# An earlier Silu, an earlier scaling of beta, and block reads on another queue, in a DeltaNet and SwiGLU kernel

## The chip, the cores and the metric

The kernel runs on one core of a Trainium2 chip. The metric is the device time of one execution in microseconds (us). The kernel before was timed three times: 864.71, 864.77 and 868.80 us, with a median of 864.77 us. The profiled execution has a span of 866.4 us.

Five engines run side by side, each through its own instructions in order: TensorE (PE; its weight loads are listed apart as PEld), VectorE (DVE), ScalarE (ACT), GpSimd (POOL) and SyncE (SP). SP, ACT and POOL also start transfers (DMA), each on its own queue.

## The reference: a delta-rule recurrence, then a gated feed-forward layer

The first half is a recurrent attention over 4 batches with 8 heads, 768 tokens and head size 48. The second half is a SwiGLU layer over the 3072 resulting rows of width 384, with an inner width of 1536. All inputs are float32 or wider; the weights arrive as 64-bit numbers.

```python
k_n = k / (norm(k) + 1e-06)
for t in range(S):
    y[:, :, t] = q[:, :, t] @ state
    v_old = state^T k_n[:, :, t]
    state += beta[:, :, t] * outer(k_n[:, :, t], v[:, :, t] - v_old)
x  = y rearranged to (3072, 384)
xn = x / sqrt(mean(x * x) + 1e-06) * rms_g
g  = xn @ w_gate
out = (g * sigmoid(g) * (xn @ w_val)) @ w_out
```

The gate product `g` goes through Silu, the value product does not, and their product is what the last matrix multiplies.

## The kernel before: the parts that matter here

The sequence is cut into six chunks of 128 tokens; with four batches there are 24 units, unit n being chunk n // 4 and batch n % 4. For each chunk the kernel computes scores of keys and queries, inverts a small triangular matrix per block (`invert`), runs the recurrence (`recur`) and then the feed-forward layer for two pairs of batches (`ffn`). These routines are Python generators. A plan with a time for each of them takes them forward in turn, so that the work of one chunk's attention lies between the matrix products of another chunk's feed-forward layer.

```python
with tc.manual_schedule():
    first = recur(0, 1.2, begin())
    next(first)
    at(1, first)
    run_plan(60)      # every engine keeps the order written
run_plan()            # from here on the scheduler orders each engine's instructions
```

One step `f` of the feed-forward layer makes 128 of the 1536 inner columns. Gate and value go into the two halves of one PSUM tile of 2 KB in each partition, of which there are two.

```python
for f in range(f0, f1):
    p_gv = psum.tile([128, 2, TOK], FP32, name="p_gv", tag="gv", bufs=2)
    for i in range(2):                      # 0: gate, 1: value
        for t in range(KT):
            nc.tensor.matmul(p_gv[:, i], wgv_sb[...], xt[:, t], ...)
        yield 1
    sil = work.tile([128, TOK], FP32, name="sil")
    nc.scalar.activation(out=sil, in_=p_gv[:, 0], func=ACTF.Silu)
    h_f = work.tile([128, TOK], FP32, name="h_f", bufs=3)
    nc.vector.tensor_tensor(out=h_f, in0=sil, in1=p_gv[:, 1], op=ALU.mult)
    if last is not None:
        leave(f - 1, last)                  # p_o += h_f of the step before, times w_out
        yield 1
    last = h_f
yield 0.9
leave(f1 - 1, last)
```

The preparation of a unit ends with its scores, which ScalarE copies and VectorE masks, and with four transfers that gather the diagonal blocks. The inversion of a chunk begins with the scaling of beta.

```python
def prepare(n):
    norm_k(n, square_k(n, nc.scalar)); yield 4
    transpose(n, qpad[n % 2], Q0); ... yield 3
    transpose(n, kpad[n % NK], K0); yield 2
    score(n, ..., both); yield 1
    gather(n)                               # four ScalarE-issued transfers

def scale_beta(c):                          # four VectorE instructions
    nc.vector.tensor_scalar_add(nrm, nrm, 1e-6)
    nc.vector.reciprocal(krec, nrm)
    for i in range(2):
        nc.vector.tensor_tensor(out=beta_t[:, c], in0=beta_t[:, c], in1=krec, op=ALU.mult)

def invert(c, dt):
    clear_ttb()
    scale_beta(c)
    turn_beta(c)                            # p_nb on TensorE, then nbeta on VectorE
    for b in range(B):
        scale_v(B * c + b)                  # GpSimd
    yield dt
    for i in range(W - 1):                  # 31 steps of two VectorE instructions
        ...  # tmp = gblk * nbeta * ttb ; ttb += tmp
        yield dt
```

The weights are turned from 64-bit to 32-bit numbers in the first 160 us by `convert`, five VectorE instructions for each piece (`top`, `wgv_sb` and `wo_sb` in the profile). In chunk 0 the inverse blocks go through memory: `td` and `nd` are written and read back by `read_two`, for batches 0 and 1 first and for 2 and 3 later.

```python
# chunk 0 of recur, cut
corner(None, 0); corner(None, 1)
read_two(2, *inverses)          # eight reads of 64 KB, all issued by SyncE
fetch(nc.sync.dma_start)        # a piece of weights
for n in (2, 3): load_v(n)
load_k(B)
...                             # inner, outer
transpose_y(0, scale(*ys.pop(0)))
stay_warm(2)
transpose_y(1, scale(*ys.pop(1)))
convert(4)
yield
```

Of the kernel before, what the change touches and what calls it, by code (L numbers as in the profile page):

```python
# [10 lines left out]
FP32 = mybir.dt.float32  # L11
# [17 lines left out]
def kernel(  # L29
# [401 lines left out]
    def prepare(n):  # L431
        norm_k(n, square_k(n, nc.scalar))
        yield 4
        transpose(n, qpad[n % 2], Q0)
        if n + 2 < NU:
            load_q(n + 2)
        yield 3
        transpose(n, kpad[n % NK], K0)
        yield 2
        score(n, crossed((0, slice(0, 3)), (1, slice(1, 4))), both)  # L440
        yield 1
        gather(n)


    def score_part(n, first):
# [83 lines left out]
        nc.scalar.dma_start(out=nd, in_=gblk)  # L529
        return td, nd  # L530

    def read_two(n, td, nd):
        own = slice(n * H, (n + 2) * H)
        both = ((td, tt_all[:, own]), (nd, ne_2))

        for d, to in both[:: -1 if n > 0 else 1]:
            for a in range(NBLK):
                o, first = W * (a % 2), a * BH + n * H
                (nc.sync if n > 0 or a < 2 else nc.scalar).dma_start(
                    out=to[W * a : W * (a + 1), :, o : o + W],  # L540
                    in_=d[first : first + 2 * H].rearrange("h r j -> r h j"),
                )

    def invert(c, dt):
        clear_ttb()
        scale_beta(c)
        turn_beta(c)
        for b in range(B):
            scale_v(B * c + b)
        yield dt  # L550
        for i in range(W - 1):
            n = W - 1 - i
            shape = [128, i + 1, n]
            tmp_b = work.tile([128, W * W // 4], FP32, name="tmp")
            tmp = tmp_b[:, 0 : n * (i + 1)].rearrange("p (k j) -> p k j", j=n)
            nc.vector.scalar_tensor_tensor(  # L556
                out=tmp,
                in0=gblk[:, i, None, i + 1 :].to_broadcast(shape),
                scalar=nbeta[:, i : i + 1],
                in1=ttb[:, 0 : i + 1, i : i + 1].to_broadcast(shape),  # L560
                op0=ALU.mult,
                op1=ALU.mult,
            )
            to = ttb[:, 0 : i + 1, i + 1 :]
            nc.vector.tensor_tensor(out=to, in0=to, in1=tmp, op=ALU.add)  # L565
            yield dt
        td = dram.tile([128, W, W], FP32, name="td")
        nc.sync.dma_start(out=td, in_=ttb)

        nd = dram.tile([128, W, W], FP32, name="nd")  # L570
        nc.vector.tensor_tensor(
            out=gblk,
            in0=ttb.rearrange("p s m -> p m s"),
            in1=nbeta[:, :, None].to_broadcast([128, W, W]),
            op=ALU.mult,
        )
        nc.sync.dma_start(out=nd, in_=gblk)
        for b in range(B):
            for a in range(NBLK):
                o = W * (a % 2)  # L580
                nc.sync.dma_start(
                    out=tt[b][W * a : W * (a + 1), :, o : o + W],
                    in_=td[a * BH + b * H : a * BH + (b + 1) * H].rearrange("h r j -> r h j"),
                )
            for a in (0, 2):
                nc.sync.dma_start(
                    out=ne[W * a : W * (a + 1), b * H : (b + 1) * H],
                    in_=nd[a * BH + b * H : a * BH + (b + 1) * H].rearrange("h r j -> r h j"),
                )
        yield dt  # L590
# [13 lines left out]
    def recur(c, dt, inverses=None):  # L604
# [204 lines left out]
        if c == 0:  # L809

            halved = [halves(b) for b in units]
            next(halved[0])
            next(halved[1])
            next(halved[0])
            next(halved[1])
            corner(0, None)
            corner(1, None)
            convert(2)
            corner(None, 0)
            corner(None, 1)  # L820
            read_two(2, *inverses)
            fetch(nc.sync.dma_start)
            for n in (2, 3):
                load_v(n)
            load_k(B)
            convert(3)
            inner(0, None, 0)
            inner(1, None, 1)
            inner(None, 0, None)
            inner(None, 1, None)  # L830
            convert(1)
            u_0, u_1 = us[0], us[1]
            stay_warm(1)
            outer(None, 0)
            outer(None, 1)
            for i in range(4):
                fetch(nc.gpsimd.dma_start)
            convert(3)
            stay_warm(3)
            transpose_y(0, scale(*ys.pop(0)))  # L840
            stay_warm(2)
            transpose_y(1, scale(*ys.pop(1)))
            convert(4)
            yield
            update(0, u_0)
            scale_v(2)
            scale_v(3)
            mask_queries(2)
            yield dt
            update(1, u_1)  # L850
            reload()
            yield dt
            next(halved[2])
            mask_queries(3)
            yield dt
            next(halved[3])
            yield dt
            next(halved[2])
            yield dt
            corner(2, None)  # L860
            next(halved[3])
            yield dt
            corner(3, 2)
            yield dt
            inner(None, None, 2)
            corner(None, 3)
            yield dt
            inner(2, None, 3)
            yield dt
            inner(3, 2, None)  # L870
            yield dt
            u_2, u_3 = us[2], us[3]
            outer(None, 2)
            yield dt
            inner(None, 3, None)
            yield dt
            outer(None, 3)
            yield dt
            transpose_y(2, scale(*ys.pop(2)))
            yield dt  # L880
            transpose_y(3, scale(*ys.pop(3)))
            yield dt
            update(2, u_2)
            yield dt
            update(3, u_3)
            reload()
            return
# [30 lines left out]
    def scale(y, p_y, rs):  # L918
        nc.scalar.mul(y, p_y.rearrange("p h d -> p (h d)"), rs)
        return y  # L920
# [18 lines left out]
    def ffn(m, f0, f1):  # L939
        xt = xts[m] if f1 < FT else xts.pop(m)  # L940
        p_o = [psum.tile([128, DM], FP32, name="p_o", tag="out", bufs=2) for i in range(2)]

        def leave(f, h_f):
            for i in range(2):
                nc.tensor.matmul(  # L945
                    p_o[i],
                    h_f[:, i * C : (i + 1) * C],
                    wo_sb[:, f],
                    start=(f == f0),
                    stop=(f == f1 - 1),  # L950
                )

        last = None
# [4 lines that stand above are left out]
                    nc.tensor.matmul(  # L958
                        p_gv[:, i],
                        wgv_sb[:, i * KT + t, f * 128 : (f + 1) * 128],  # L960
                        xt[:, t],
                        start=(t == 0),
                        stop=(t == KT - 1),
                    )
                yield 1
            sil = work.tile([128, TOK], FP32, name="sil")
            nc.scalar.activation(out=sil, in_=p_gv[:, 0], func=ACTF.Silu)  # L967
            h_f = work.tile([128, TOK], FP32, name="h_f", bufs=3)
            nc.vector.tensor_tensor(out=h_f, in0=sil, in1=p_gv[:, 1], op=ALU.mult)  # L969
            if last is not None:  # L970
                leave(f - 1, last)
# [5 lines that stand above are left out]
            n = 2 * m + i  # L977
            if f0 == 0:
                o_sb = work.tile([128, DM], FP32, name="o_sb", bufs=4)
                nc.scalar.copy(o_sb, p_o[i])  # L980
            else:
                o_sb = halves.pop(n)
                nc.vector.tensor_tensor(out=o_sb, in0=o_sb, in1=p_o[i], op=ALU.add)
            if f1 < FT:
                halves[n] = o_sb
                continue
            c, b = divmod(n, B)
            tok0 = b * S + c * C
            nc.sync.dma_start(out=out[tok0 : tok0 + C, :], in_=o_sb)
        yield 0.1  # L990
# [16 lines left out]
    def begin():  # L1007
# [31 lines left out]
            keep_queries(n, score_part(n, Q0))  # L1039
        tops.append(shrink(raws[1]))  # L1040
        inverses = invert_halves()
        read_two(0, *inverses)
        stay_warm(4)
        stay_warm(8, ttb_all[:, 0:DM].rearrange("p (t m) -> p t m", m=128))
        mask_queries(0)
# [57 lines left out]
```

## Time and profile before

| engine | busy us | share of the span | instructions |
| --- | --- | --- | --- |
| PE | 832.2 | 96% | 8640 |
| PEld | 638.7 | 74% | 8640 |
| DVE | 411.9 | 48% | 1000 |
| ACT | 251.7 | 29% | 655 |
| POOL | 107.0 | 12% | 146 |

The share of an engine over the whole span hides its stages. In the page's 40 slices of 21.7 us the DVE stands at 7 to 9 tenths in the first eight slices and then falls to between 1 and 7, while the PE stands at 9 in nearly all. The groups of instructions that the change touches are these:

| group | count | mean of one | busy us |
| --- | --- | --- | --- |
| p_gv products, 128x256 (PE) | 1728 | 386 ns | 416.1 |
| p_o products, 128x384 (PE) | 576 | 502 ns | 217.7 |
| sil (ACT) | 144 | 383 ns | 55.1 |
| h_f (DVE) | 144 | 418 ns | 60.2 |

Each float32 product of the program is two instructions in the trace, so one step `f` has six instructions for the gate, six for the value and four for `p_o`. "Idle before" in a row of the timeline is the time for which the engine had nothing to run just before that instruction, and the arrow names what ended it.

### The profile page before, as it was taken

Reading aid. Unit: us, or ns where it says so; the run is one execution under the profiler, and the core shown is the slowest. Engines: PE = TensorE matmul, PEld = TensorE weight load, DVE = VectorE, ACT = ScalarE, POOL = GpSimd, SP = SyncE. Lnnn points to the kernel's source line nnn. Section 1 sums busy time; section 2 is a strip of 40 time slices with the busy share of each in tenths; the row PEclk is TensorE's granted clock in tenths of the full one; section 3 lists DMA queues with packets and bytes.
Section 4 is the critical chain, followed back from the end, with each engine's and each line's share of the span. In section 5 each row is a group of like instructions: output and inputs, shape, how many; then the busy total and the mean of one; then the engine's idle time right before and its main releaser. Section 6 shows DMA issues by size and latency. Waiting matters only on the chain.

```text
span 866.4 us, 20251 instructions
## 1 busy us (share of the span) xinstructions
PE 832.2 (96%) x8640; PEld 638.7 (74%) x8640; DVE 411.9 (48%) x1000; ACT 251.7 (29%) x655; POOL 107.0 (12%) x146
## 2 busy tenths in 40 slices
PE   7898979689999999999999999999999999999998
PEld 6576757467887777877777887777777777777776
DVE  7869969791443761343661442671333581220100
ACT  5344446003334113244113244112334112220101
POOL 6012433100230000230000230000130000000000
PEclk9969999899999999999999999999999999999999
DMA  8846345104221131221121222122121122000000
GB/s 152 231 99 211 121 122 144 31 24 90 48 62 34 32 84 28 48 62 32 31 83 32 43 61 37 31 78 38 39 57 19 31 71 35 2 20 0 19 1 18
DMA packets 152058, 52.01 MB, mean 60 GB/s; under 512 B 143616, under 2 KB 146688, under 8 KB 151968
## 3 DMA queue, kind: packets, MB, share of 16 engines
q1 hardware_dynamic: 124816, 36.95, 18.5%
q0 software_dynamic: 2080, 10.23, 3.5%
q10 hardware_dynamic: 25072, 3.54, 2.3%
q8 instruction: 68, 1.11, 0.5%
q14 instruction: 22, 0.18, 0.1%
HBM read 36.54 MB, written 14.16 MB: 59 GB/s over the span
## 4 chain that ended last, share of the span: by engine, by line
PE 79%; DVE 15%; issue 2%; ACT 2%; DMA 1%; POOL 1%; SPq 0%; DVEq 0%; ACTq 0%; POOLq 0%
PE p_gv L958 38%; PE p_o L945 18%; DVE tmp L556 4%; DVE ttb L565 3%; PE p_g L373 3%; PE p_y L715 3%; PE p_z L771 2%; PE p_t L357 2%; PE p_k L753 2%; PE p_y L753 2%; PE p_z L780 1%; PE p_x L789 1%; PE p_v L620 1%; PE p_w L627 1%; DVE h_f L969 1%
## 5 line engine op out<-in xcount | busy, mean ns | idle before, releaser
L958 PE MATMUL p_gv<-xt,wgv_sb 128*128 128x256 f32 x1728 | 416.1, 386 | 1.3 <-DVE xt L929 0.7
L958 PEld LDWEIGHTS p_gv<-xt,wgv_sb 128*128 128x128 f32 x1728 | 321.5, 191 | 66.0 <-issue 4.3
L945 PE MATMUL p_o<-wo_sb,h_f 128*128 128x384 f32 x576 | 217.7, 502 | 9.0 <-DVE h_f L969 9.0
L969 DVE TENSOR_TENSOR h_f<-sil,p_gv 128x256 f32<-128x256 f32 x144 | 60.2, 418 | 247.3 <-ACT sil L967 247.2
L967 ACT ACTIVATE sil<-p_gv 128x256 f32<-128x256 f32 x144 | 55.1, 383 | 335.8 <-PE p_gv L958 314.4
L945 PEld LDWEIGHTS p_o<-wo_sb,h_f 128*128 128x128 f32 x576 | 105.0, 192 | 61.2 <-DVE h_f L969 13.8
L556 DVE SCALAR_TENSOR_TENSOR tmp<-gblk,nbeta,ttb 128x31 f32<-128x31 f32 (+15 forms) x155 | 62.7, 405 | 4.7
L387 DVE TENSOR_TENSOR gp<-p_g,mask 64x128 f32<-64x128 f32 (+1 forms) x160 | 37.9, 277 | 43.2 <-ACT gp L383 38.7
L565 DVE TENSOR_TENSOR ttb<-ttb,tmp 128x31 f32<-128x31 f32 (+15 forms) x155 | 53.0, 342 | 4.9
L320 POOL TENSOR_TENSOR knrm<-ksum,half 128x8 f32<-128x8 f32 x24 | 41.8, 1741 | 71.0 <-DVE ksum L319 70.8
L914 POOL TENSOR_SCALAR ms<-ms 128x1 f32<-128x1 f32 x24 | 5.3, 221 | 312.0 <-ACT y L906 311.7
L362 ACT COPY kqt<-p_t 128x512 f32<-128x512 f32 x48 | 28.1, 585 | 24.9 <-PE p_t L357 24.2
L489 POOL MEMSET ttb<- 128x1024 f32 x6 | 5.7, 954 | 228.9 <-DMA td<-ttb 228.9
L771 PEld LDWEIGHTS p_z<-v_raw,tt 64*64 64x64 f32 x768 | 26.0, 142 | 9.2 <-issue 7.2
L373 PE MATMUL p_g<-kqt 64*64 64x192 f32 x640 | 31.7, 330 | 0.9 <-ACT gp L383 0.9
L640 ACT COPY vs<-p_v 32x256 f32<-32x256 f32 x48 | 17.4, 362 | 44.4 <-PE p_w L627 23.2
L780 PE MATMUL p_z<-u,x 64*64 64x48 f32 x384 | 28.8, 227 | 0.7 <-DVE u L801 0.6
L789 PE MATMUL p_x<-tt,gp 64*64 64x64 f32 x384 | 29.0, 229 | 0.2 <-issue 0.2
L771 PE MATMUL p_z<-v_raw,tt 64*64 64x48 f32 x768 | 29.2, 227 | 0.0
L373 PEld LDWEIGHTS p_g<-kqt 64*64 64x64 f32 x640 | 23.1, 132 | 8.1 <-issue 5.3
L715 PE MATMUL p_y<-u,gp 128*64 128x48 f32 x768 | 27.6, 228 | 0.0
L780 PEld LDWEIGHTS p_z<-u,x 64*64 64x64 f32 x384 | 25.7, 142 | 2.4 <-issue 1.3
(117 smaller groups left out, 784.1 us busy)
## 6 DMA issues: line engine op xcount, KB each, us to landing
kpad<-in_k_dram SPq DMA_DIRECT2D x24, 192.0 KB, 2.9
qpad<-in_q_dram SPq DMA_DIRECT2D x24, 192.0 KB, 2.9
v_raw<-in_v_dram SPq DMA_DIRECT2D x24, 192.0 KB, 2.9
out_dram<-o_sb SPq DMA_DIRECT2D x24, 192.0 KB, 1.9
gblk<-gd SPq DMA_DIRECT2D x6, 512.0 KB, 3.3
td<-ttb SPq DMA_DIRECT2D x6, 512.0 KB, 2.6
raw<-in_moe_w_val_dram POOLq DMA_DIRECT2D x8, 384.0 KB, 4.3
raw<-in_moe_w_out_dram POOLq DMA_DIRECT2D x8, 384.0 KB, 4.3
```

The costliest lines, as they stand in the source:

```text
L320: nc.gpsimd.tensor_tensor(out=norms[c][:, b * H : (b + 1) * H], in0=ksum, in1=half, op=ALU.pow)
L373: nc.tensor.matmul(to, pair[d, K1 if i else K0], pair[d, places], skip_group_check=True)
L387: nc.vector.tensor_tensor(out=to[p, :, place], in0=p_g[p, :, place], in1=mask[p, i, None].to_broadcast([p.stop, 2, HC]), op=ALU.mult,)
L556: nc.vector.scalar_tensor_tensor(out=tmp, in0=gblk[:, i, None, i + 1 :].to_broadcast(shape), scalar=nbeta[:, i : i + 1], in1=ttb[:, 0 : i ...
L565: nc.vector.tensor_tensor(out=to, in0=to, in1=tmp, op=ALU.add)
L715: nc.tensor.matmul(p_y[p, h], gp[b_y][:, h, HC * place : HC * (place + 1)], u[:, h], start=(c == 0 and h == 0), stop=True, skip_group_chec ...
L771: nc.tensor.matmul(p_zs[b_z][p, h], tt[b_z][p, h], r[p, h], start=(h == 0), stop=(p is lo), skip_group_check=True,)
L780: nc.tensor.matmul(p_zs[b_u][hi, h], x2s[b_u][:, h], us[b_u][lo, h], start=False, stop=True, skip_group_check=True,)
L945: nc.tensor.matmul(p_o[i], h_f[:, i * C : (i + 1) * C], wo_sb[:, f], start=(f == f0), stop=(f == f1 - 1),)
L958: nc.tensor.matmul(p_gv[:, i], wgv_sb[:, i * KT + t, f * 128 : (f + 1) * 128], xt[:, t], start=(t == 0), stop=(t == KT - 1),)
L967: nc.scalar.activation(out=sil, in_=p_gv[:, 0], func=ACTF.Silu)
L969: nc.vector.tensor_tensor(out=h_f, in0=sil, in1=p_gv[:, 1], op=ALU.mult)
```

## The change

There are three parts. The Silu of a step is issued straight behind its gate product, ahead of the value product, where it used to stand behind both. The scaling of a chunk's beta moves from the head of the inversion to the end of the preparation of the chunk's last unit, for every chunk from the second on. Of the eight block reads for batches 2 and 3 of the first chunk, SyncE keeps one, and ScalarE issues the other seven later, behind the scaling of `y`; `read_two` takes a list of queues for that. The first part is to have the Silu done while TensorE works on the value product; the second is to have beta ready when the inversion asks for it; the third is to free SyncE's queue earlier for the transfers behind the reads.

```diff
 # prepare
         yield 1
         gather(n)
+        if n % B == B - 1:
+            scale_beta(n // B)
 # read_two: takes queues; None leaves a read out, and a short list ends it
-    def read_two(n, td, nd):
+    def read_two(n, td, nd, queues):
 # invert
         clear_ttb()
-        scale_beta(c)
         turn_beta(c)
 # recur, chunk 0
             corner(None, 1)
-            read_two(2, *inverses)
+            read_two(2, *inverses, [nc.sync])
             fetch(nc.sync.dma_start)
 ...
             transpose_y(1, scale(*ys.pop(1)))
+            read_two(2, *inverses, [None] + 7 * [nc.scalar])
             convert(4)
 # ffn
                         stop=(t == KT - 1),
                     )
+                if i == 0:
+                    sil = work.tile([128, TOK], FP32, name="sil")
+                    nc.scalar.activation(out=sil, in_=p_gv[:, 0], func=ACTF.Silu)
                 yield 1
-            sil = work.tile([128, TOK], FP32, name="sil")
-            nc.scalar.activation(out=sil, in_=p_gv[:, 0], func=ACTF.Silu)
             h_f = work.tile([128, TOK], FP32, name="h_f", bufs=3)
 # begin: the same queues as before
-        read_two(0, *inverses)
+        read_two(0, *inverses, 2 * [nc.sync, nc.sync, nc.scalar, nc.scalar])
```

The order of the reads in `read_two(2, ...)` is as before: the four of `nd` first, then the four of `td`.

More of the change, by code (lines that the diff above doesn't have):

```diff
@@ L530, in invert_halves @@
         return td, nd
-    def read_two(n, td, nd):
+    def read_two(n, td, nd, queues):
         own = slice(n * H, (n + 2) * H)
[L534 to L542, printed above, removed]
+        reads = [(d, to, a) for d, to in ((td, tt_all[:, own]), (nd, ne_2)) for a in range(NBLK)]
+        if n > 0:
+            reads = reads[NBLK:] + reads[:NBLK]
+        for (d, to, a), queue in zip(reads, queues):
+            if queue is None:
+                continue
+            o, first = W * (a % 2), a * BH + n * H
+            queue.dma_start(
+                out=to[W * a : W * (a + 1), :, o : o + W],
+                in_=d[first : first + 2 * H].rearrange("h r j -> r h j"),
+            )
     def invert(c, dt):
         clear_ttb()
-        scale_beta(c)
         turn_beta(c)
```

## The prediction

> **What bounds the kernel now.** I read four views in this order. First the table of windows, because an average over the span hides the stages. Its columns are the stretch, its length, then busy time and instruction count of PE, PEld, DVE, ACT and POOL, the granted PE clock, the DMA share and the GB/s.
>
> ```profile
> 150.00:160.00 10.00, 3.69 (x14) 2.21 (x13) 9.69 (x22) 1.76 (x6) 1.48 (x2) 0.98 0.25 66
> 160.00:170.00 10.00, 9.67 (x36) 7.39 (x37) 4.78 (x16) 1.34 (x3) 1.71 (x3) 0.68 0.01 2
> ...
> 260.00:392.00 132.00, 131.26 (x1402) 101.26 (x1401) 57.38 (x156) 37.95 (x105) 14.05 (x18) 1.00 0.21 47
> 392.00:524.00 132.00, 131.27 (x1398) 101.17 (x1397) 57.38 (x156) 37.94 (x105) 14.05 (x18) 1.00 0.21 47
> ```
>
> There are two regimes. From about 200 us on, TensorE is busy 131.3 of each 132 us: nothing that speeds another engine up can shorten that part, and whatever makes TensorE wait adds in full. Before 193 us VectorE is the tight engine in most slices. The stretch from 150 to 160 us is the one large hole: TensorE 3.69 us busy, VectorE 9.69.
>
> Second, the list of waits of TensorE, over the whole span and then from 200 us on:
>
> ```profile
> PE p_o L945 <- DVE h_f L969: 9.0, 7, 2.7
> PE p_nb L337 <- DVE beta_t L331: 4.8, 1, 4.8
> PE p_xt L928 <- ACT y L919: 3.5, 2, 2.3
> ...
> PE p_o L945 <- DVE h_f L969: 2.9, 4, 0.7
> ```
>
> The columns are total us, number, longest. The waits that parts one and two aim at are 9.0 and 4.8 us; of the 9.0 only 2.9 us lie in the steady part. That is the ceiling of what can be won there.
>
> Third, the timeline around the hole:
>
> ```profile
> 153.52 0.40 DVE L969 TENSOR_TENSOR h_f<-sil,p_gv 128x256 f32<-128x256 f32 x1
> ...
> 157.88 0.41 DVE L969 TENSOR_TENSOR h_f<-sil,p_gv 128x256 f32<-128x256 f32 x1
> 158.21 0.17 DVE L327 TENSOR_SCALAR knrm<-knrm 128x32 f32<-128x32 f32 x1
> ...
> 158.81 1.37 DVE L331 TENSOR_TENSOR beta_t<-beta_t,krec 128x32 f32<-128x32 f32 x2
> 160.33 0.33 PE L337 MATMUL p_nb<-ident,beta_t 32*32 32x32 f32 x8 [4.79 <-DVE beta_t L331]
> 160.59 2.93 PE L945 MATMUL p_o<-wo_sb,h_f 128*128 128x384 f32 x4
> ...
> 167.64 0.38 ACT L967 ACTIVATE sil<-p_gv 128x256 f32<-128x256 f32 x1 [3.61 <-PE p_gv L958]
> 168.06 0.42 DVE L969 TENSOR_TENSOR h_f<-sil,p_gv 128x256 f32<-128x256 f32 x1 [4.20 <-ACT sil L967]
> ```
>
> The reader is to see that two things end at nearly the same time: h_f at 158.3 and beta at 160.2, one behind the other on VectorE, with conversion of weights ahead of both. TensorE needs both, beta for p_nb and this h_f for the p_o that stands behind p_nb.
>
> Fourth, the steady part, to see what Silu waits for and how the scheduler orders TensorE:
>
> ```profile
> 295.93 2.75 PE L958 MATMUL p_gv<-xt,wgv_sb 128*128 128x256 f32 x12
> 298.52 1.45 PE L945 MATMUL p_o<-wo_sb,h_f 128*128 128x384 f32 x4
> 298.72 0.38 ACT L967 ACTIVATE sil<-p_gv 128x256 f32<-128x256 f32 x1 [3.50 <-PE p_gv L958]
> 300.24 0.41 DVE L969 TENSOR_TENSOR h_f<-sil,p_gv 128x256 f32<-128x256 f32 x1
> 300.71 1.56 PE L945 MATMUL p_o<-wo_sb,h_f 128*128 128x384 f32 x4 [0.73 <-DVE h_f L969]
> ...
> 320.31 0.24 PE L620 MATMUL p_v<-tt,gp 32*32 32x32 f32 x2
> 320.48 1.56 PE L958 MATMUL p_gv<-xt,wgv_sb 128*128 128x256 f32 x6
> 321.97 0.69 PE L620 MATMUL p_v<-tt,gp 32*32 32x32 f32 x30
> ```
>
> Silu starts 0.04 us after the twelfth product (295.93 + 2.75 = 298.68), though it reads only what the first six wrote. And the 32 products of p_v, one run in the source, are parted by a gate: the scheduler puts other ready work where an instruction is not ready.
>
> **What the Trainium skill says.** "PSUM — Partial Sum Buffer", section "PSUM bank collisions raise a hardware error", says that two engines must not touch one bank in the same 32 partitions at a time, whatever the columns. Gate and value share one bank, so an early Silu and the value products have to exclude each other: the value product will wait for the Silu. The trace agrees as far as it can: Silu waits for all twelve. "TensorE: Matmul & The Clock Gate", section "What's actually happening", says that an idle window of about 3.4 us halves the clock; the trace shows 0.68 granted in 160 to 170 us, behind the 4.79 us hole. "DMA: Bandwidth & Descriptors", section "Issuing engines are not separate DMA queues", says that another issuing engine saves only issue time, as the same DMA engines carry the data; no view of before tests that.
>
> **Beta.** Nothing is added or removed: 0.17 + 0.35 + 1.37, about 2.0 us of VectorE with gaps, move ahead of some conversion, by roughly the distance between the last scores' masks (end 153.6) and 158.2. Then beta is ready at about 156 and TensorE, which reaches p_nb at 155.54, hardly waits there. But the h_f of 157.88 now has those 2.0 us ahead of it and ends at 158.3 + 2.0 = 160.3, so the p_o behind p_nb starts at about 160.35 instead of 160.59. The wait changes its name. What stays as a gain is VectorE's own 0.54 us before nbeta, as p_nb has long been done: the inversion starts at 160.5 instead of 161.0. VectorE orders the stage from there to 193 us, so about 0.5 us is won. In later chunks beta is long ready and nothing changes.
>
> **Silu, in the written order (to about 195 us).** h_f no longer follows value, Silu (0.38) and a hop, but value and a hop: 0.42 us earlier against the value's end. The value product, where it follows its gate directly, starts 0.04 + 0.38 + 0.05, about 0.5 us later. The two cancel, for VectorE. The two places where Silu stood behind other ScalarE work help (h_f at 126.29 was ready to start 1.5 us earlier, the value product having ended at 124.75), but the masks at 130.61 wait for scores in TensorE's stream anyway. Against it, TensorE now hangs on ScalarE's order: the first Silu has a conversion copy that waits for a transfer until 67.2 and a table load of 1.28 us ahead of it, so the first value product starts some 3 us later. TensorE's later waits for VectorE (1.54, 0.79, 0.65, 0.64 us up to 98 us) take that up. Sum for this part: 0 to +1 us.
>
> **Silu, under the scheduler.** The value product is not ready when its gate ends; p_o of the step before is. I expect the order gate(f), p_o(f-1), value(f), which hides 0.46 us of Silu under 1.3 us of p_o. The cost then is lost slack. Before, h_f had p_o, gate and value, 1.3 + 2.6 us, from the value's end; now it has one gate, 1.3 us, of which hop and h_f take 0.46, leaving 0.84. In the inversion h_f comes up to 1.14 us late (Silu ended at 299.10, h_f began at 300.24), so a few tenths per step are lost over a few steps: 0.5 us a chunk. Silu has 0.84 us too, and ScalarE's four gathers hold its queue for 1.8 us (256.00 to 257.8): perhaps 1.5 hits a chunk at 0.7 us, 1 us a chunk. Over four chunks, 2 + 4 us. Back come up to 2.9 us of old h_f waits, say 1.5, because TensorE can be given another gate there. At the very end value, hop, h_f and p_o lie in a row: +0.4 us. Sum about +3 us, a rough estimate.
>
> **The reads.** SyncE issued four reads of nd at 48.54 to 51.64 and four of td at 51.69 to 53.77; one stays, so the weights, v and k behind them start about 5 us earlier. Nothing waits for these: VectorE has no transfer among its waits. ScalarE gets seven issues of about 0.45 us, 3.2 us, from about 63.3, in a hole of 3.93 us in which it waits for weights. The reads land by about 70, and p_vh, which needs them, runs at 72.66. 448 KB now run beside the four weight fetches, which may come 1 to 2 us later; VectorE needs the first at 72.1. Sum 0 to +0.5 us.
>
> **Sum.** -0.5, +0.5, +3 and +0.3 would be 868. I take off 1.5, since both slack losses are guesses of the unkind sort: 866.5 us.
>
> **Rivals.** (1) The scheduler does not reorder. Then every value product that follows its gate directly pays 0.5 us: about eleven in each 132 us by the timeline, some 65 in all, +32 us, 897. For: the last stretch from 788 us has nothing to fill with but p_o. Against: the parted p_v. I give it 7%. (2) The 4.8 us hole closes really, because the conversions behind the moved beta are not needed for that h_f. Then the clock stays up too: p_o took 2.93 instead of 1.45 and the 24 p_gv behind it 6.89 instead of 5.34, so up to 4.8 + 3 us, 857. Against: VectorE has 9.69 of 10 us to do and is in order. 10%. (3) ScalarE's queue turns into the pace: gathers and score copies (eight of 0.27 us) stand before Silu more often than I count, +10 us, 875. 13%.
>
> **Range and chances.** 860 to 878 holds the main case, most of (3) and part of (2). 2% is 17.3 us: only (1), or a bad (3), goes beyond it, 0.09; nothing in the profile offers 17 us to win, 0.02.
>
> **What would show it.** Right: p_nb has a wait below 1 us and p_o behind it one of about 4; the order gate, p_o, value in the last stretch; TensorE still at 131 of 132 us or a little less, with new waits of p_gv for sil. Wrong: TensorE waits of 0.5 us for sil in the last stretch (rival 1); more than 7 us busy between 150 and 160 us (rival 2).

## The result, and the profile after

The changed kernel takes 889.28 us, the median of four runs (886.81 to 891.84); the kernel before takes 865.53 us in its four (864.71 to 868.80). The ratio is 1.0267, with a 95% interval of 1.0226 to 1.0309. The change costs 23.7 us, and the predicted range ended at 878.

The table of windows of the changed kernel, with the columns of the one before:

```profile
150.00:160.00 10.00, 8.62 (x64) 6.17 (x62) 9.76 (x21) 4.39 (x12) 0.83 (x2) 1.00 0.20 40
160.00:170.00 10.00, 5.67 (x23) 3.37 (x22) 8.25 (x18) 0.96 (x2) 3.50 (x4) 0.83 0.16 53
...
260.00:392.00 132.00, 130.65 (x1360) 97.96 (x1358) 56.44 (x153) 36.63 (x100) 14.08 (x18) 1.00 0.20 46
392.00:524.00 132.00, 130.66 (x1379) 97.57 (x1379) 56.38 (x153) 36.56 (x101) 12.43 (x17) 1.00 0.21 47
```

By its busy share TensorE has lost almost nothing in the steady part: 130.65 of 132 us, where it was 131.26. The counts say otherwise: VectorE finishes 153 instructions in the stretch instead of 156, ScalarE 100 instead of 105. The weight loads fall from 101.2 to 97.6 us of 132, and that is the first honest sign. The Trainium skill says so in general ("Perfetto Trace Analysis", section "Identifying the Most-Contended Engine": the busy time of products is a poor measure of how near TensorE is to its limit, because they are pipelined, and that of weight loads a good one), and this case agrees. The hole of 150 to 160 us has moved on by about 6 us; it has not closed: TensorE now waits 0.70 us for beta and then, until 166.26 us, 3.62 us for h_f, where it waited 4.79 us at one place.

The list of TensorE's waits, over the whole span:

```profile
PE p_gv L963 <- ACT sil L972: 14.0, 17, 7.0
PE p_o L950 <- DVE h_f L975: 7.6, 9, 3.6
PE p_xt L933 <- ACT y L924: 4.2, 3, 2.4
PE p_g L458 <- ACT kqt L362: 3.6, 2, 3.4
PE p_vh L677 <- DMA tt<-td: 2.5, 1, 2.5
```

and that of the weight loads from 200 us on:

```profile
PEld p_gv L963 <- ACT sil L972: 28.0, 65, 0.9
PEld p_o L950 <- DVE h_f L975: 9.7, 11, 1.1
```

The first row of each list is new. Of its 14.0 us, 12.9 lie before 200 us, so the list of products shows only 1.2 us of it in the steady part; there it is the weight load that waits for the Silu, 65 times. A product that starts late but had another one running ahead of it does not count as waiting.

Where the time is lost can be read from the start of each inversion (`nbeta`), which marks a chunk:

| | chunk 1 | 2 | 3 | 4 | 5 | chunk lengths |
| --- | --- | --- | --- | --- | --- | --- |
| before | 160.71 | 285.62 | 417.06 | 549.09 | 681.18 | 124.9, 131.4, 132.0, 132.1 |
| after | 166.12 | 291.14 | 425.53 | 561.35 | 697.17 | 125.0, 134.4, 135.8, 135.8 |

There are two losses. About 5.5 us are there before the first of these marks and stay; from the second mark on, each chunk takes 3.0 to 3.8 us more, and the last stretch adds the rest. Followed by h_f, the 21st comes 5.7 us late (at 210.6 us), the last 22.1.

The early loss begins here, in the timeline of the changed kernel:

```profile
65.68 7.75 ACTq L544 DMA_DIRECT2D tt<-td  x4
...
67.69 1.56 PE L963 MATMUL p_gv<-xt,wgv_sb 128*128 128x256 f32 x6 [0.65 <-DVE xt L934]
...
73.56 0.90 ACT L244 ACTIVATE top<-wgv_sb 128x768 f32<-128x768 f32 x1 [8.63 <-DVE wo_sb L279]
74.47 1.28 ACT L972 ACT_TABLE_LOAD   x1
...
75.76 0.38 ACT L972 ACTIVATE sil<-p_gv 128x256 f32<-128x256 f32 x1
76.20 2.21 PEld L963 LDWEIGHTS p_gv<-xt,wgv_sb 128*128 128x128 f32 x6 [7.36 <-ACT sil L972]
76.20 2.93 PE L963 MATMUL p_gv<-xt,wgv_sb 128*128 128x256 f32 x6 [6.95 <-ACT sil L972]
```

The first gate is done at 69.25. ScalarE is still issuing the last four reads, which hold its queue for 7.75 us, until 73.43; a conversion copy and a table load follow, then the Silu, then the value product. (The label at the copy names a conversion of VectorE, which ended at 73.10, before the issues did.) TensorE stands for 6.95 us, and runs the six value products in 2.93 instead of 1.56 us after that.

The later loss is a small thing many times. The last stretch of the kernel before, and then of the changed kernel:

```profile
822.67 2.75 PE L958 MATMUL p_gv<-xt,wgv_sb 128*128 128x256 f32 x12
825.05 1.05 PEld L945 LDWEIGHTS p_o<-wo_sb,h_f 128*128 128x128 f32 x4
825.26 1.45 PE L945 MATMUL p_o<-wo_sb,h_f 128*128 128x384 f32 x4
825.47 0.38 ACT L967 ACTIVATE sil<-p_gv 128x256 f32<-128x256 f32 x1 [3.50 <-PE p_gv L958]
...
826.55 2.75 PE L958 MATMUL p_gv<-xt,wgv_sb 128*128 128x256 f32 x12
```

```profile
843.53 1.46 PE L963 MATMUL p_gv<-xt,wgv_sb 128*128 128x256 f32 x6
844.61 0.41 PEld L950 LDWEIGHTS p_o<-wo_sb,h_f 128*128 128x128 f32 x2
844.82 0.81 PE L950 MATMUL p_o<-wo_sb,h_f 128*128 128x384 f32 x2
845.02 0.38 ACT L972 ACTIVATE sil<-p_gv 128x256 f32<-128x256 f32 x1 [3.91 <-PE p_gv L963]
845.46 1.16 PEld L963 LDWEIGHTS p_gv<-xt,wgv_sb 128*128 128x128 f32 x6 [0.44 <-ACT sil L972]
845.47 1.55 PE L963 MATMUL p_gv<-xt,wgv_sb 128*128 128x256 f32 x6
846.86 0.81 PE L950 MATMUL p_o<-wo_sb,h_f 128*128 128x384 f32 x2
...
847.50 1.46 PE L963 MATMUL p_gv<-xt,wgv_sb 128*128 128x256 f32 x6
```

Before, a step goes from gate to gate in 3.88 us (822.67 to 826.55); after, in 3.97 (843.53 to 847.50). The scheduler does put `p_o` between gate and value, but only half of it, two of its four instructions. That is 0.65 us, and the Silu is done 0.58 us after their start: the value's first weight load can't run ahead of the products any more, but starts at 845.46, with the first product right behind it. In this undisturbed stretch the exposed load costs 0.09 us a step. Among the attention's work the loss is larger: a chunk of 24 steps takes 3.8 us more, 0.16 us a step.

### The profile page after: what moved, and what is told of

It is laid out like the page before. It is cut to its first block, busy times and chain, and to the rows that moved or that the text cites. A ratio compares the mean times of both kernels' runs of the same rounds, so it can differ in the third digit from the quotient of the medians.

```text
span 888.4 us, 20360 instructions
## 1 busy us (share of the span) xinstructions
PE 847.3 (95%) x8640; PEld 633.3 (71%) x8640; DVE 411.2 (46%) x1000; ACT 252.2 (28%) x655; POOL 106.5 (12%) x146
## 4 chain that ended last, share of the span: by engine, by line
PE 76%; DVE 2%; ACT 1%; issue 1%; POOL 1%; DMA 0%; POOLq 0%; DVEq 0%; ACTq 0%
PE p_gv L963 39%; PE p_o L950 20%; PE p_g L373 3%; PE p_y L719 2%; PE p_k L757 2%; PE p_y L757 2%; PE p_z L775 2%; PE p_t L357 1%; PE p_v L624 1%; PE p_x L793 1%; PE p_w L631 1%; PE p_z L784 1%; ACT sil L972 1%; DVE tmp L560 1%; PE p_s L738 1%
## 5 line engine op out<-in xcount | busy, mean ns | idle before, releaser
L963 PE MATMUL p_gv<-xt,wgv_sb 128*128 128x256 f32 x1728 | 437.5, 390 | 15.5 <-ACT sil L972 14.0
L963 PEld LDWEIGHTS p_gv<-xt,wgv_sb 128*128 128x128 f32 x1728 | 315.0, 191 | 109.6 <-ACT sil L972 45.4
L950 PE MATMUL p_o<-wo_sb,h_f 128*128 128x384 f32 x576 | 226.4, 500 | 7.8 <-DVE h_f L975 7.6
L911 ACT ACTIVATE y<-p_y 128x384 f32<-128x384 f32 x24 | 11.8, 491 | 70.1 <-PE p_y L719 70.0
```

Source lines behind the costliest of these rows:

```text
L950: nc.tensor.matmul(p_o[i], h_f[:, i * C : (i + 1) * C], wo_sb[:, f], start=(f == f0), stop=(f == f1 - 1),)
L963: nc.tensor.matmul(p_gv[:, i], wgv_sb[:, i * KT + t, f * 128 : (f + 1) * 128], xt[:, t], start=(t == 0), stop=(t == KT - 1),)
```

## The experiments

Each kernel was timed beside the kernel before on its chip; medians of before were 866.3 to 866.7 us there. A profile is one execution, and its first 205 us vary from one to the next: two kernels below that take the same time as before reach that point 3.3 us ahead of it and 1.6 us behind it. From there to the last h_f, those two and the kernels with the reads or the beta alone agree with the profile of before within 0.8 us.

**The three parts, each alone.** First the Silu alone, the changed kernel with the other two parts taken back:

```diff
-        if n % B == B - 1:
-            scale_beta(n // B)
+        scale_beta(c)                       # at the head of invert again
-            read_two(2, *inverses, [nc.sync])
+            read_two(2, *inverses, 8 * [nc.sync])
-            read_two(2, *inverses, [None] + 7 * [nc.scalar])
```

> The kernel before with the early Silu alone. Theory: the loss has two sources. In the steady part each value product's first weight load stands behind the Silu and is not taken in under the half p_o ahead of it, 0.09 us a step in the last stretch and about 0.13 to 0.15 with attention between, so some 16 us from 200 us on; in the written order 0.47 us for each of the eight steps from 165 to 200 us, mostly hidden by VectorE. The start is nearly spared, since ScalarE has no block reads ahead of the first Silu: that Silu waits for the copy of weights that lands at 67 us and for the table load, 3 us, which later waits take up. So 880 to 883 us. Rival: the early Silu costs only where ScalarE's queue is held by other issues, that is by the reads at the start, and the rest is the reads' and the scaling's doing: then 866 to 869.

Measured: 882.17 us (881.86 to 883.76), ratio 1.0186 [1.0153, 1.0220]. The theory held. Up to 205 us this kernel is 2.0 us ahead of before, which is within the spread of profiles; its first value product waits 2.8 us for the Silu. From there to the last h_f it loses 16.2 us, as the changed kernel does (16.4).

The reads alone, with Silu and beta in their old places:

> The kernel before with the late reads on ScalarE alone. Theory: ScalarE's queue is held by the issues until about 73 us and the reads land at about 78 us, but with Silu behind both products no product waits for Silu at the start, so the first products run on; what is left is the copy of weights 5 us late and p_vh, which needs the blocks at 72.7 us and gets them at 76 to 78: 2 to 4 us, 867 to 870. Rival: the reads do their whole harm, 5.5 us, without Silu, by landing beside the weights: 871. Second rival: they are free, 865.

Measured: 873.92 us (870.61 to 874.56), 1.0080 [1.0052, 1.0108]. The first rival was right in kind, and its 871 was passed: the reads do harm without the early Silu. TensorE's waits there (first rows):

```profile
PE p_vh L676 <- DMA tt<-td: 9.9, 3, 7.8
PE p_o L949 <- DVE h_f L973: 7.5, 6, 2.7
```

The `tt` reads held ScalarE's queue for 9.41 us and landed 14.8 us after issue (2.4 before), and `p_vh` waited for them. In the changed kernel the wait for the Silu takes the place of most of this wait.

Beta alone:

> The kernel before with the earlier scaling of beta alone. Theory: the wait of p_nb (4.8 us) falls below 1 us and the p_o behind it waits for h_f instead, about 3.6 to 4.4 us; the inversion starts 0.5 us earlier; 864.5 to 865.5. Rival: the hole closes, the clock stays up and 5 to 8 us are won: 858 to 860.

Measured: 867.62 us (862.52 to 869.98, 12 runs), 1.0010 [0.9993, 1.0027]: no difference, and not the small gain that was expected. Its waits of TensorE:

```profile
PE p_o L949 <- DVE h_f L973: 12.9, 8, 3.6
...
PE p_nb L337 <- DVE beta_t L331: 1.9, 1, 1.9
```

The wait for beta falls from 4.8 to 1.9 us, and one of 3.6 us for h_f appears behind it: the same hole with another name. The three parts alone make 15.8, 7.6 and 1.3 us, 24.7 in all, where the whole change makes 23.7. That they add up so well is partly chance, as the last of the experiments shows.

**The Silu: is it the shared bank?** The Silu stays early, but gate and value get a bank each, with one buffer each, so that the banks needed are the same:

```diff
-            p_gv = psum.tile([128, 2, TOK], FP32, name="p_gv", tag="gv", bufs=2)
+            p_gv = [psum.tile([128, TOK], FP32, name=f"p_gv{i}", tag=f"gv{i}", bufs=1) for i in range(2)]
 # and p_gv[:, i] becomes p_gv[i]; p_t, which shared the tag, alternates between gv0 and gv1
```

> The early Silu alone, but gate and value in a bank of their own each (one buffer each in place of two shared ones). Theory: the value product waits for Silu only because the two share a bank, and everything that the early Silu loses from 165 us on comes from that order. With own banks the value product follows its gate at once, the steady part goes back to 131.3 us busy and about 132 us a chunk, and what the early Silu wins before 165 us (it stood 3.1 us ahead there when alone) stays: 862 to 866 us. Rival: the loss is the scheduler's other order or ScalarE's queue, and not the shared bank: still 875 to 882. Second rival: a single buffer for each makes the next gate or value wait for Silu or h_f: above 870.

Measured: 865.28 us (861.75 to 869.68, 12 runs), 0.9996 [0.9975, 1.0017]. The theory held: 16.9 us less than with the shared bank, with the Silu where it was, and the loss that single buffers might have brought did not show in the time. Each half is now also a tile of its own; one tile over two banks was not tried, so the runs do not tell the sharing of a bank from the sharing of a tile. The last stretch of this kernel:

```profile
827.29 2.75 PE L961 MATMUL p_gv<-xt,wgv_sb 128*128 128x256 f32 x12
828.78 0.38 ACT L970 ACTIVATE sil<-p_gv 128x256 f32<-128x256 f32 x1 [3.50 <-PE p_gv L961]
829.88 1.45 PE L948 MATMUL p_o<-wo_sb,h_f 128*128 128x384 f32 x4
831.17 2.75 PE L961 MATMUL p_gv<-xt,wgv_sb 128*128 128x256 f32 x12
```

The Silu runs from 828.78 to 829.16 in the middle of twelve products in a row, which take 2.75 us as before; this is the overlap that the change was after, and the step is 3.88 us again. The profiles agree on this: the three full chunks together are 10.2 to 10.5 us longer than before in all four kernels with the early Silu and the changed kernel's order on a shared bank, and 1.6 us shorter in all three with own banks. Those 1.6 us are too little to show in the times: TensorE sets the pace, and before 200 us a new wait, the value or gate product for the h_f that frees its single buffer, takes 7.7 us in five places.

**Is it the order of TensorE?** With the Silu early and the bank shared, the whole of `p_o` is written between gate and value:

```diff
                     nc.scalar.activation(out=sil, in_=p_gv[:, 0], func=ACTF.Silu)
+                    if last is not None:
+                        leave(f - 1, last)
                 yield 1
...
             if last is not None:
-                leave(f - 1, last)
                 yield 1
```

> The early Silu alone, shared bank as in the changed kernel, but the whole p_o of the step before is written between gate and value (1.29 us in place of the half, 0.65 us, which the scheduler chose). Theory: the loss in the steady part is that Silu ends 0.46 us after the gate and that the half p_o leaves no time to load the value's first weights behind it; under a whole p_o they are loaded in time. The loss of 14 us from 200 us on falls to the waits for h_f, 1 to 3 us, and the 0.47 us waits in the written order go: 864 to 869. Rival: it is the lost slack of h_f (one gate in place of a p_o and two products), which is the same here: 878 to 882.

Measured: 884.26 us (881.16 to 888.69), 1.0218 [1.0174, 1.0261]. The expectation fell, and the rival's figure was passed too. In the last stretch the wait is indeed hidden, with steps of 3.88 us; but among the attention's work the chunks take 136.2 us. There the Silu stands behind ScalarE's other work (value products that follow `p_xt`, whose `y` is ScalarE's, start 3.1 us later over three chunks), and h_f is wanted one product earlier: `p_o` waits 18 times for it in this kernel, against 7 before. A wait that is hidden where ScalarE is free is not hidden where it is busy.

The opposite: Silu in its old place, without any wait of value for Silu, but with `p_o` parted around the value product as the scheduler does it:

```diff
 # leave takes the halves of p_o to write
+                if i == 0 and last is not None:
+                    leave(f - 1, last, (0,))      # first half of p_o
                 yield 1
...
-                leave(f - 1, last)
+                leave(f - 1, last, (1,))          # second half
```

> The kernel before, Silu behind both products as there, but p_o in two halves, one ahead of the value product and one behind it: TensorE's order in the last stretch is that of the changed kernel, without a wait for Silu. Theory (the cost is the wait for Silu ahead of a weight load): as before, 865 to 868. Rival (the cost is the finer change between p_o and p_gv itself, 0.1 us at each change): about +0.1 to 0.2 us for each of 144 steps, 880 and more.

Measured: 877.25 us (876.39 to 878.97), 1.0135 [1.0105, 1.0166], between theory and rival. Before 205 us it loses 5.4, where this order is forced on every engine. From there to the last h_f it loses 5.6: 2.8 up to the mark of chunk 2, where the changed kernel loses nothing, 1.8 in the three full chunks and 1.0 behind them, where the changed kernel loses 10.5 and 6.1. The weight loads of `p_o` wait 9.8 us for h_f from 205 us on, against 5.9 before. In the last stretch it runs at 3.88 us a step, so parting `p_o` costs nothing by itself. Of the 16 us that the early Silu costs from the mark of chunk 2 on, an earlier `p_o` thus makes about 3, and the wait of the value product for the Silu about 13, if the two simply add, which no run shows.

**The reads: who issues them, or when?** The late reads alone, by ScalarE, but ahead of the squares of `y` (at 53 to 59 us instead of 63 to 74):

```diff
+            read_two(2, *inverses, [None] + 7 * [nc.scalar])
             outer(None, 0)
             outer(None, 1)
...
-            read_two(2, *inverses, [None] + 7 * [nc.scalar])   # behind transpose_y
```

> The late reads alone, again by ScalarE, but placed ahead of the squares of y, where ScalarE has nothing to do from about 53 to 59 us and no weights are under way. If the 7.6 us of the late reads are their meeting with the weight fetches that start at 62.5 us (they landed 12 to 15 us after their issue, against 2.4 before), they land by 59 us and the time is that of before, 865 to 867. If it is the issuing engine, ScalarE's queue itself, 2 us or more stay: 868 to 874.

Measured: 865.72 us (862.48 to 869.65, 20 runs), 0.9996 [0.9979, 1.0013], as expected if the meeting with the fetches did the harm. And the late reads alone in their late place in the program, with SyncE as the issuer:

> The late reads alone, at the late place of the program but issued by SyncE, which has no data to wait for there and issues them at about 57 to 62 us (as in the profile of the changed kernel with SyncE), ahead of the weights. Theory (it is when the reads run, not who issues them or where they stand): 865 to 867. Rival: 870 and more, as the timed runs of the changed kernel with SyncE (889, no gain) suggest.

Measured: 865.86 us (863.82 to 869.41, 12 runs), 0.9994 [0.9974, 1.0015], and the theory held. The transfer lists of the reads-only kernels, ScalarE late, ScalarE earlier, and SyncE, in this order (KB each and us from issue to landing at the end):

```profile
tt<-td ACTq DMA_DIRECT2D x4, 64.0 KB, 14.8
```

```profile
tt<-td ACTq DMA_DIRECT2D x4, 64.0 KB, 4.5
```

```profile
tt<-td SPq DMA_DIRECT2D x4, 64.0 KB, 2.5
```

Neither ScalarE as the issuer nor a late line in the program does harm: SyncE, which has nothing else to wait for, issues early from the late line too. The harm goes with the time at which the reads run: only the late ones of ScalarE meet the large weight fetches that GpSimd issues from some 62 to 64 us on; in 68 to 78 us the transfer engines are busy all the time, in the changed kernel as in the one before. That agrees with the Trainium skill, "DMA: Bandwidth & Descriptors", section "Issuing engines are not separate DMA queues": all issuers share the same transfer engines. What it calls usually small beside the transfer, the time to issue, was not small here: 7.75 us for four reads, which ScalarE's other work had to wait out. It is not ScalarE's alone: in the kernel before, SyncE took 0.37 us to issue a transfer of k at 69.18 us, and 2.81 us for the next one, beside the same fetches, at 71.28 us. Why the issue itself stretches was not tried, and no run has SyncE issue the reads at the later time, so whether ScalarE makes it worse there stays open.

**Putting the mended parts together.** The changed kernel with own banks, reads left late:

> The changed kernel with banks of their own for gate and value and nothing else undone, reads late as they are. Theory: what is left is the cost of the late reads alone, 7.6 us: 872 to 875. Rival (the wait of the first value product for Silu behind ScalarE's issues is a cost of its own, beside the reads'): the first value product waits no more, so p_vh's wait for the blocks takes its place and the time is the same; if the two added up, it would be 866 to 869.

Measured: 868.45 us (863.81 to 876.42, 20 runs), 1.0036 [1.0014, 1.0058]. That is within the second range, and some 3 us by the ratio, less than the 7.6 of the reads alone. Own banks thus take away some 20 of the 23.7 us with the late reads still in place. The first value product no longer waits, but the next gate does, since the gate has one buffer and the Silu has not read it:

```profile
76.38 2.93 PE L963 MATMUL p_gv<-xt,wgv_sb 128*128 128x256 f32 x6 [5.14 <-ACT sil L972]
```

The start loses 4.5 us by 103 us, and in this profile most of it is won back by 205 us (0.8).

The changed kernel with own banks and the earlier reads:

> The changed kernel with both faults mended: gate and value in banks of their own, and the seven reads by ScalarE ahead of the squares of y, before the weight fetches. Theory (the parts are independent and their costs were the shared bank and the meeting of transfers): about 24 us below the changed kernel, 863 to 866, and the steady part about 0.5 us a chunk shorter than before, since the waits of p_o for h_f went with own banks (393.9 in place of 395.6 us for three chunks), so 0 to 2.5 us below the kernel before. Rival (the parts interact): above 868.

Measured: 869.17 us (862.59 to 877.18, 19 runs), 1.0009 [0.9990, 1.0029]. The run of 877.18 us, over 1.5% above the fastest of this kernel, does not count in the ratio. The loss is gone, but the expected gain did not come: no version here beats the kernel before.

**The reads in the changed kernel.** With its shared bank, once with SyncE as the issuer of the seven late reads, once with ScalarE's earlier reads (edits as above):

> The changed kernel, with the seven late reads issued by SyncE at the same place instead of by ScalarE. If the harm at the start is ScalarE's queue being held (issues of 7.8 us ahead of the copy, the table load and the first Silu), then the wait of the first value product falls from 7.0 to about 2.5 us and the time falls by 3 to 5 us, to 884 to 886. If the harm is that the reads land late beside the weights, the wait only moves to p_vh and the time stays at 888 to 890.

> The changed kernel as it is (shared bank, early Silu, early beta), but the seven reads by ScalarE stand ahead of the squares of y, where alone they cost nothing. Theory (the three costs add): the reads' 7.6 us go, 880 to 884 us, the first Silu done before 71 us, h_f number 20 no later than 3 us against before's 204.87, and chunks of about 135.5 us behind it. Rival (as in the timed runs of the kernel with SyncE's late reads, where nothing came back): 887 to 891 us, with the loss appearing behind 200 us instead, or the reads landing late after all.

Measured: 889.19 us (883.93 to 891.09), 1.0253 [1.0211, 1.0295], and 887.90 us (886.38 to 889.24), 1.0242 [1.0215, 1.0269]. In neither do the 7.6 us come back: the first lands on the figure for late reads, though the reads of its profile had landed by 64.6 us, and in the second the rival was right. The second profile shows one way. Its reads land after 4.7 us, and at 103 us it is level with before (0.2 us late); but at 138 us it is 4.7 us late again. ScalarE's timeline there:

```profile
124.21 0.38 ACT L972 ACTIVATE sil<-p_gv 128x256 f32<-128x256 f32 x1 [1.80 <-PE p_gv L963]
124.21 3.49 ACTq L405 DMA_DIRECT2D gd<-gp  x4
127.75 0.64 ACT L748 COPY state<-p_s 64x192 f32<-64x192 f32 x2 [3.16 <-issue]
128.41 0.89 ACT L244 ACTIVATE top<-raw 128x768 f32<-128x768 f32 x1
129.32 0.59 ACT L362 COPY kqt<-p_t 128x512 f32<-128x512 f32 x1
129.81 0.39 ACT L972 ACTIVATE sil<-p_gv 128x256 f32<-128x256 f32 x1
```

and TensorE's:

```profile
126.54 1.46 PE L963 MATMUL p_gv<-xt,wgv_sb 128*128 128x256 f32 x6
127.93 0.67 PE L738 MATMUL p_s<-u,kpad 128*64 128x48 f32 x16
130.25 2.64 PE L963 MATMUL p_gv<-xt,wgv_sb 128*128 128x256 f32 x6 [1.65 <-ACT sil L972]
```

The gate is done at 128.0; four gathers hold ScalarE's queue until 127.70 (3.49 us, where the same four took 1.87 in the profile with SyncE's reads), the copies that had piled up go ahead, and the value product waits for the Silu until 130.25 and then runs at a lower clock (0.57 granted in 130 to 134 us). With own banks and the earlier reads the same gathers hold ScalarE's queue for 2.93 us, and the Silu is late too, but the value product starts at 125.84 us, ahead of it:

```profile
121.52 2.93 ACTq L405 DMA_DIRECT2D gd<-gp  x4
126.60 0.39 ACT L972 ACTIVATE sil<-p_gv 128x256 f32<-128x256 f32 x1
```

So the early loss was not a property of the reads alone: with the early Silu on a shared bank, a delay of ScalarE's queue stops TensorE, here by reads and there by gathers. The one profile with SyncE's reads (883.93 us) shows neither delay and is 0.9 us ahead of before at 205 us; its three timed runs are slower by 5 to 7 us. Whether the gathers were held in those can't be seen, and stays open. No run has the early Silu and the early beta with the reads as before, so an interplay of these two isn't excluded either.

## Why the prediction was wrong

**Beta: the waits were right, the small gain was not.** The prediction had `p_nb` wait under 1 us, `p_o` behind it some 4, and half a microsecond won. The changed kernel shows 0.70 and 3.62 us (beta alone 1.89 and 3.62), but nothing won: from the 11th h_f to nbeta both kernels take 7.65 us, where before took 7.19. Two conversions behind the moved beta run 1.23 and 1.47 us there, 0.56 and 0.96 before, beside GpSimd's scaling of v, which had moved ahead too. Rival 2, a hole that really closes, fell.

**The failed step is the Silu under the scheduler.** The prediction said "I expect the order gate(f), p_o(f-1), value(f), which hides 0.46 us of Silu under 1.3 us of p_o" and put the whole at about 3 us (its own terms, 2 and 4 less 1.5 and 0.4 on top, make 4.9). Measured from 205 us on: 16.2 to 16.4. Half of the mechanism was seen: that two engines have to keep off one bank at a time, whichever half they use (the Trainium skill, "PSUM — Partial Sum Buffer", section "PSUM bank collisions raise a hardware error"), so that the value product waits for the Silu; the kernel with own banks shows what that wait costs, 16.9 us. What was missed is that the wait would not be hidden:

- The scheduler put half of `p_o` there, 0.65 us, just what the Silu needs and no more. The value's weight load, which otherwise runs under the product ahead, then stands in the open.
- Hidden in the last stretch is not hidden among attention work. Even with all of `p_o` between, the order that the prediction expected, the chunks were 136.2 us long.

The term for the lost slack of h_f, 2 us, was about right: the kernel that keeps the Silu's place and only parts `p_o` loses 2.8 from the mark of chunk 2 on.

The three full chunks are 10.5 us longer than before. Counting each TensorE instruction's start from the start of the one ahead of it, less the usual distance (0.22 us behind a product of `p_gv`, 0.32 behind one of `p_o`), the trace gives about 3.7 us more ahead of the value product, 3.1 within it, 2.2 at `p_o` and 1.5 elsewhere: two thirds stand at the value product. The prediction's rival 1 had the value product wait for the Silu each time, which is right, but because the scheduler would not reorder, which is wrong, and at 0.5 us a step and 32 us it had twice the size. Rival 3, ScalarE's queue as the pace, came in part at the start, but little in the steady part: in those three chunks the Silu starts more than 0.1 us after its gate in 15 of 72 steps, and the value product comes straight behind such a late Silu in 7.

**Written order: right while nothing else delays ScalarE.** The wait per directly following value product is 0.47 us in the changed kernel (at 170.99 and 174.32, for example), as predicted, and the early Silu alone shows no loss up to 205 us. The first value product's delay, taken as 3 us and absorbed, was 2.8 us with the Silu alone and 6.95 in the changed kernel, because of the reads in front of it. (The value product that the prediction has end at 124.75 us ended at 124.91; nothing hangs on it.)

**The reads were the second failed step.** "The reads land by about 70" and "0 to +0.5 us": they held ScalarE to 73.4 us instead of 3.2 us from 63.3, landed after 12.2 us, and cost 7.6 us alone. With own banks and the early Silu some 3 us of that are left; why not all 7.6 is not shown. The prediction took the issue times of an idle stretch (0.45 us each) and the landing of 2.4 us, and saw that 448 KB would run beside the weight fetches, but asked only whether the fetches would come later, not whether the reads would.

**The signs named beforehand** would have misled: "TensorE still at 131 of 132 us or a little less" held, and was given as a sign of being right; so did, by half, "the order gate, p_o, value in the last stretch". The sign of rival 2, "more than 7 us busy between 150 and 160 us", came true with 8.62 us, only because the hole had moved out of that window. The busy share of the products fell by 0.6 us in 132 here, where the chunk grew by 3.8.

## What to carry to other kernels

Before an operation is moved ahead to overlap with a product, look at which bank it reads: if the product writes the same one, the two take turns, and the engine that was slack becomes a link in TensorE's chain; give them a bank each first (here a tile each as well). A transfer's issue belongs to the in-order work of its engine, and its cost must be taken from the stretch in which it will run, beside what will run with it, not from where it ran before. Where TensorE is full, measure start to start over one period of the loop; here its busy share hid a loss of 2.9% a chunk.

## What the runs showed of the hardware

- Issue time is not a constant. Four reads of 64 KB occupied ScalarE's queue for 4.16 us at 54.8 us and for 7.75 and 9.41 us beside large fetches, and landed after 4.5, 12.2 and 14.8 us; the same four gathers took 1.87 us in one kernel's profile and 3.49 in another's.
- A weight load that waits for another engine costs even where the products show no idle time: six products take 1.55 us with the load behind the Silu and 1.46 with it ahead, and a step 3.97 us in place of 3.88.
- A wait of 1.65 us behind a stretch of thin work was followed by six products in 2.64 us, one of 6.95 us by six in 2.93, where six take 1.46 to 1.56 at the full clock. These two waits cost TensorE more than their own length.
